# A later assumed landing for the gathers of softmax sums, in the scheduler of a fused attention and feed-forward kernel

## The chip, the cores and the metric

The kernel runs on one core of a Trainium2 chip. The metric is the device time of one execution in microseconds (us). The core's engines work side by side and meet through semaphores: PE (TensorE) multiplies matrices, with PEld its weight loads; DVE (VectorE), ACT (ScalarE) and POOL (GpSimd) do elementwise work; SP (SyncE) issues most DMAs. Each engine has one stream of instructions, with waits between them, so an instruction that waits holds up all that stands behind it in its stream.

## The reference, cut to what matters

```python
# q, k, v: (8, 12, 448, 64); w_in: (768, 2048); w_out: (2048, 768)
q_n = q / (norm(q) + 1e-6);  k_n = k / (norm(k) + 1e-6)
scores = q_n @ k_n.T / tau                    # 448 x 448 for each of 96 heads
attn = exp(scores - max) / sum(exp(scores - max))
x = (attn @ v) -> (3584, 768)                 # heads side by side
h = x @ w_in
out = (h * cos(h)) @ w_out
```

## The kernel before, in words

**The work.** The 96 heads are 48 pairs (called groups, g = 0 to 47); three groups make a unit (u = 0 to 15), two units a batch (b = 0 to 7). For a group, POOL squares q and k (L629), DVE sums the squares (L636, "red"), ACT makes the norms' reciprocals (Ln at L657, Exp at L660), POOL scales (L668, "scale"), and the result is transposed by a DMA on SP (L685, T9 to T47). PE computes the scores in four steps (L719 and L727, SCg.0 to SCg.3), ACT their exponentials (L734), and PE the product with v (L760, L767, L793) and, by columns of ones, the softmax sums (L775, L783). DVE (L850) or ACT (L847) copies both from PSUM to the buffer `xu`.

**The chain of a unit** (function `chain`, L884 to L911) then divides by the sums:

1. *gather* (L888, four DMAs on SP): the sums go from `xu` into a compact tile `sums`;
2. *sum* (L900) and *recip* (L903) on DVE, each a small instruction;
3. *spread* (L904, SP): the reciprocals go to DRAM;
4. *bcast* (L906, two DMAs on SP): they come back, repeated over partitions, as `RB`;
5. *x* (L910, POOL): one multiplication for each group gives `xT`, bf16.

Some groups ("direct": 9, 10, 11, 17, 23, 47 among the later ones) make their reciprocal on ACT (L873) and need no chain. Unit 2's sum and reciprocal run on POOL.

**The feed-forward part.** For a batch, M1 (L918) multiplies six tiles of `xT` with w_in, 16 steps of six matmuls; ACT takes the cosine (L947), DVE multiplies (L949, "g"). The first two pairs of steps run early over the first three tiles (the even unit's), then over the fourth, the fifth and the sixth (the odd unit's). M2 (L1016; in quarters of 64 by 64) multiplies with w_out and is cut into small pieces that fill PE's time between the attention steps; its PSUM bank, MP, is drained by two DVE copies ("osb", L983), and only then may the next tile of M2 begin. The outputs leave by DMAs on SP (L987).

**What sets the order.** The order on PE and of most ACT work follows a script written out by hand. For the other engines, a planner in the kernel (`Program.play`, L180 on) simulates all engines once with a cost for each operation, and each engine takes, among what is ready in this simulation, the operation that is due first. `Program.emit` writes the instructions in the simulated order of starts. A DMA's landing is modelled; `pad` is added to it for whoever waits for it (`latency`):

```python
    def latency(self, y, o):
        if y.dma is not None:
            return y.pad
```

The gather's pad comes from the plan:

```python
        dma("SP", [...], [("xs", i, p) for p in range(n)], [("sums", i)], "sums%d" % i, 0.7,
            "gather%d" % u, pad=0.0 if u in PLAN["power"] else PLAN["late"])
```

With `"late": 0.0` the planner lets a sum start as soon as the modelled gather has landed. `PLAN["rush"]` is a bias on the due time of one unit's sum and recip: unit 11 is given 3 us less. `PLAN["queue"]` fixes a few orders on SP beyond what the planner finds: T34 behind spread 9, T40 behind spread 11, T46 behind spread 13; out 11 behind bcast 9, out 15 behind bcast 11, out 18 behind bcast 13.

Of the kernel before, what the change touches and what calls it, by code (L numbers as in the profile page):

```python
# [14 lines left out]
    "apart": 1,  # L15
    "ahead": (1, 2),
    "hurry": {2: -8},
    "rush": {11: -3},
    "swapped": {},
    "script": {19: """  # L20
        s19.0 f5 s19.1 f4 s19.2 f6 s19.3 f6 a18 f4 b18 s20.0 c18 c19
# [27 lines left out]
    "v3": (7, ("xa", 2, 0)),  # L49
    "late4": {2: (7, "T9")},  # L50
    "power": (2,),
    "late": 0.0,
    "mixed": (3, (3, 0, 1, 2, 0, 1, 2, 0), (2, 3, 4, 0, 1, 5)),
    "turned": 9,
    "first": (3, 1, 2, 0, 3, 1, 2, 0),
# [359 lines left out]
def bass_cosine_attention__then__act_gcu_kernel(  # L415
# [13 lines left out]
    UP = 3  # L429
# [156 lines left out]
    def load(u, p0, p1, apart=False, eng="SP", behind=None, reads=()):  # L586
        i = u % 2
        h = slice(2 * p0, 2 * p1)
        f = [lambda e, x=x, t=t: e.dma_start(
            rawv[i][BP * x : BP * x + BP, h].rearrange("p h s d -> p h (s d)"), src(t, u, 2 * p0, 2 * (p1 - p0)))  # L590
            for x, t in enumerate((k, q))]
        for x in ((0,), (1,)) if apart else ((0, 1),):
            behind = P.ops[-1] if x == (1,) else behind
            dma(eng, [f[y] for y in x], list(reads), [("raw", i, p, y) for p in range(p0, p1) for y in x] + (["first"] if (u, p0) == (0, 0) and 1 in x else []),
                "raw%d_%d_%s" % (i, p0, x), 0.97 * (p1 - p0) * len(x), "load u%d p%d" % (u, p0), behind, 1.8,
                pad=LATE if u > 1 else 0.0)
# [328 lines left out]
    def m1(b, early=0, split=NKC, turn=TURN, order=tuple(range(NKC)), done=0, inner={}):  # L925
        table(SINSET)

        def names(gi):
            return BANKS.get(PHs[turn[gi]][0], [PHs[turn[gi]][0]])

        def step(gi, a, c0, c1):
            m1_step(b, turn[gi], 2 * gi + a, c0, c1, order)

        for gi in range(done):
            for a in range(2):
                step(gi, a, NKC - 2, NKC - 1)
        for c0, c1 in [(0, split)] + [(c, c + 1) for c in range(split, NKC - 1)]:
            for gi in range(done, early):
                for a in range(2):
                    step(gi, a, c0, c1)  # L940
        for gi in range(NF // 2):
            for g in inner.get(gi, ()):
                transposes(g)
            ph, cz = PHs[turn[gi]][1], gi % 2
            for a in range(2):
                step(gi, a, NKC - 1 if gi < early else 0, NKC)
            act(lambda e, ph=ph, cz=cz: e.activation(cosv[cz], ph[:, :, 0:S], ACT.Sin, bias=cst.ap()[:, 0:1], scale=1.0),  # L947
                names(gi) + ["cst0"], [("cos", cz)], 2 * S, "S", 1, label="sin%d.%d" % (b, gi))
            dve(lambda e, ph=ph, cz=cz, gi=gi: e.tensor_tensor(  # L949
                gTv[:, 2 * gi : 2 * gi + 2, S * (b % 2) : S * (b % 2) + S], ph[:, :, 0:S], cosv[cz], ALU.mult),  # L950
                names(gi) + [("cos", cz)], [("gT", b % 2, gi)], 2 * S, label="g%d.%d" % (b, gi))
        table(EXPSET)
# [13 lines left out]
    def m2_add(b):  # L966
        for t in range((b * S) // 128, ((b + 1) * S) // 128):
            w = [0, HW, DM]
            if t == B * S // 128 - 1 and PLAN["tail"]:
                w.insert(2, HW + PLAN["tail"])  # L970
            for hf, x in enumerate(zip(w, w[1:])):
                m2_queue.append([t, hf, 0, None, x])
# [57 lines left out]
    def m2_fill(n, quarters=False):  # L1030
        while n > 0 and (m2_queue or m2_tile):
            if m2_tile or quarters and m2_queue[0][1:3] == [0, 0]:
                n -= m2_quarters(n)
                continue
            t, hf, f, bank, w = item = m2_queue[0]
            if bank is None:
                bank = item[3] = banks[0][nhalf[0] % len(banks[0])]
                nhalf[0] += 1
            name, po = bank
            col = (128 * t) % RING  # L1040
            m = min(4, n, NF - f)

            def go(e, po=po, f=f, m=m, col=col, w=w):
                for y in range(f, f + m):
                    r = e.matmul(po[:, 0 : w[1] - w[0]], gTv[:, y, col : col + 128], W2v[:, y, w[0] : w[1]],  # L1045
                                 start=(y == 0), stop=(y == NF - 1))
                return r

            P.op("PE", go, gates(t, f, m), name, cost=m * ((w[1] - w[0]) / 2400.0 + 0.0025), mode="F", label="M2 %d" % t)
            item[2] = f + m  # L1050
            n -= m
            if f + m == NF:
                m2_queue.pop(0)
                m2_drain(t, hf, name, po, w)
            elif f + m == NF - PLAN["twin"] and t == (B - 1) * S // 128 and not hf:
                m2_queue[0:2] = m2_queue[1::-1]
            elif f + m == NF - PLAN["twin"] and t == (B - 1) * S // 128:
                m2_queue[0:2] = m2_queue[1::-1]
# [21 lines left out]
    def find(label):  # L1080
        return [o for o in P.ops if o.label == label][-1]
# [23 lines left out]
    def direct(g):  # L1105
        return g in PLAN["direct"]

    def loads(u, behind=None, reads=()):
        if u < NU:
            for p in range(UP):  # L1110
                load(u, p, p + 1, behind=behind, reads=reads)
# [14 lines left out]
    def ahead_norms(g):  # L1126
        u, p = g // UP, g % UP
        if 3 <= u < NU - 1:
            if p == 0:
                norms(u + 1, 0)  # L1130
            if p == u % 2:
                norms(u + 1, 1)

    def unit_done(g):
        u = g // UP
        if g > PB and not direct(g - 1) and (g % UP == 0 or direct(g)):
            chain((g - 1) // UP)
        if g % UP == 0:
            if g > PB and (u <= 3 or u % 2 == 0):
                for x in range(UP if u + 2 < NU else 0):  # L1140
                    load(u + 2, x, x + 1, behind=find("bcast%d" % (2 if u == 4 else u - 1)) if u > 3 else
                         find(PLAN["u5"][x]) if u == 3 else None)
            if g > PB:
                for x, y in PLAN["vloads"].get(u, [(u + 2, "x%d" % (g - 1 if u % 2 == 0 else g - 4))]):
                    load_v(x, find(y))

    def play(text):
        order, phase, last = [0, 2, 1], {}, 0

        def touch(x=None):  # L1150
            x = [y for y in order if y not in [held[z] for z in phase if len(phase[z]) < 3]][0] if x is None else x
            order.remove(x)
            order.append(x)
            return x

        for w in text.split():
            kind, rest_ = w[0], w[1:]
            if kind == "o":
                order[:] = [int(x) for x in rest_]
                continue  # L1160
            if kind == "f":
                m2_fill(int(rest_), True)
                continue
            if kind == "m":
                m1(int(rest_), 2, UP, tuple(touch() for x in range(NF // 2)))
                m2_add(int(rest_))
                continue
            if kind == "s":
                g, c = (int(x) for x in rest_.rstrip("=").split("."))
                if c == 0:  # L1170
                    ahead_norms(g)
                last = touch(last if rest_[-1] == "=" else None)
                scores(g, c, last)
                if c == 1 and max(TD, PB + 2) <= g + 2 < NG:
                    transposes(g + 2)
                if c == 3 and g % UP == UP - 1 and g // UP % 2 == 0:
                    loads(g // UP + 3, find("bcast%d" % (g // UP - 1)))
                continue
            g = int(rest_)
            held[g] = touch(held.get(g))  # L1180
            if kind == "c" and g not in phase:
                turned.add(g)
            attend(g, direct(g), ({"a": 0, "b": 1, "c": 2}[kind],))
            phase[g] = phase.get(g, "") + kind
            if len(phase[g]) == 3:
                unit_done(g + 1)
# [164 lines left out]
```

## Time and profile before

| what | value |
|---|---|
| median of 3 runs (lowest to highest) | 421.99 us (420.87 to 422.92) |
| the profiled execution | 421.52 us, of which the span of its instructions 419.8 us |
| PE busy | 411.3 us, 98% of the span |
| DVE, ACT, POOL busy | 188.8, 272.1, 242.8 us |
| granted TensorE clock | 1.0 in every slice |
| DMA | 152 GB/s in the mean |

"Busy" is the time in which an engine had an instruction in work; matmuls are pipelined, so PE's share is an upper bound of its use. A wait is shown as idle time of an engine with the instruction that ended it. The span has 40 slices, and PE's row shows 9 tenths or more in all but the first, the second and the last. The chain that ended last, followed back through the whole span, is 87% PE, 4% ACT, 3% DMA, 2% POOL and 1% DVE.

### The profile page before, as it was taken

The page shows a single profiled execution, that of the slowest core. Times are in us where ns is not written, and L with a number is a line of the kernel's source. Part 1 is how long each engine was busy: PE and PEld are TensorE (multiplying, and loading weights), DVE is VectorE, ACT ScalarE, POOL GpSimd, SP SyncE. Part 2 cuts the span into 40 slices and gives each one's busy share as a digit, 9 for nine tenths or more (in the row PEclk, how much of TensorE's full clock was granted, in tenths as well). Part 3 has the DMA queues.
Part 4 walks back from the last instruction along what each step waited for, and adds up shares of the span by engine and source line. Part 5 has one row for each costly group of instructions (what it writes and reads, how often), then busy time and mean ns, then how long its engine had stood idle before and what let it go on. Part 6 is the DMA issues. An engine that isn't in the chain of part 4 may idle for free.

```text
span 419.8 us, 13605 instructions
## 1 busy us (share of the span) xinstructions
PE 411.3 (98%) x6077; PEld 236.9 (56%) x6077; DVE 188.8 (45%) x250; ACT 272.1 (65%) x363; POOL 242.8 (58%) x193
## 2 busy tenths in 40 slices
PE   8899999999999999999999999999999999999996
PEld 3454556655566555665566555665566655555555
DVE  3564744356743277124752087213862244223421
ACT  4897578984987646876598556776498645703500
POOL 4999977998941866938864684808957302020000
PEclk9999999999999999999999999999999999999999
DMA  8999999999966998789665994759936920141023
GB/s 185 251 255 226 207 220 187 207 216 154 157 100 129 231 180 172 147 182 218 153 122 114 210 250 100 124 117 221 240 89 89 187 68 2 42 121 38 2 71 81
DMA packets 81034, 63.61 MB, mean 152 GB/s; under 512 B 45776, under 2 KB 75984, under 8 KB 80976
## 3 DMA queue, kind: packets, MB, share of 16 engines
q1 hardware_dynamic: 62768, 50.06, 57.3%
q0 software_dynamic: 18048, 12.59, 20.6%
q8 instruction: 48, 0.79, 0.8%
q10 hardware_dynamic: 160, 0.10, 0.1%
q14 instruction: 10, 0.08, 0.1%
HBM read 54.98 MB, written 11.13 MB: 157 GB/s over the span
## 4 chain that ended last, share of the span: by engine, by line
PE 87%; ACT 4%; DMA 3%; POOL 2%; SPq 2%; DVE 1%; issue 0%; ACTq 0%; POOLq 0%
PE MP L1016 25%; PE SC L918 21%; PE AV L918 11%; PE SC L719 6%; PE AV L767 4%; PE MP L1045 4%; PE SC L1045 3%; PE AV L793 2%; ACT PX L734 2%; PE SC L767 2%; PE AV L760 2%; PE MP L918 2%; DMA sums<-xu 1%; DMA raw<-in_q_dram 1%; POOL qks L668 1%; ACT cosb L947 1%
## 5 line engine op out<-in xcount | busy, mean ns | idle before, releaser
L734 ACT ACTIVATE PX<-SC 128x896 bf16<-128x896 f32 (+1 forms) x166 | 132.7, 828 | 25.2 <-PE SC L719 17.7
L1016 PE MATMUL MP<-W,gT 64*64 64x384 bf16 x2816 | 142.4, 324 | 1.3 <-DVE qkT L706 0.6
L1016 PEld LDWEIGHTS MP<-W,gT 64*64 64x64 bf16 x2816 | 78.8, 107 | 37.0 <-PE MP L1016 4.3
L918 PE MATMUL SC<-xT,W 128*128 128x448 bf16 x468 | 94.9, 353 | 0.0
L668 POOL TENSOR_TENSOR qks<-raw,rn 128x896 bf16<-128x896 f32 (+1 forms) x48 | 79.7, 1677 | 23.9 <-ACT rn L660 23.3
L629 POOL TENSOR_TENSOR sq<-raw 128x896 bf16<-128x896 f32 x44 | 73.4, 1688 | 9.7 <-DMA raw<-in_q_dram 7.6
L947 ACT ACTIVATE cosb<-SC,cst 128x896 f32<-128x896 f32 x39 | 39.1, 1006 | 57.0 <-PE SC L918 51.3
L910 POOL TENSOR_TENSOR xT<-xu,RB 128x448 bf16<-128x448 f32 x34 | 37.8, 1134 | 64.6 <-DMA RB<-scr 64.6
L918 PEld LDWEIGHTS SC<-xT,W 128*128 128x128 bf16 x468 | 45.5, 98 | 42.8 <-ACT xu L847 0.6
L949 DVE TENSOR_TENSOR gT<-SC,cosb 128x896 bf16<-128x896 f32 x39 | 42.4, 1089 | 39.7 <-ACT cosb L947 37.4
L918 PE MATMUL AV<-xT,W 128*128 128x448 bf16 x264 | 56.7, 353 | 0.0
L636 DVE TENSOR_REDUCE n<-sq 128x14 f32<-128x896 bf16 (+2 forms) x49 | 51.3, 1057 | 6.2 <-ACT sq L627 5.6
L983 DVE COPY osb<-MP 128x384 f32<-128x384 f32 x50 | 25.7, 548 | 57.4 <-PE MP L1016 46.8
L719 PE MATMUL SC<-qkT 64*64 64x448 bf16 x504 | 45.9, 356 | 0.6 <-ACT PX L734 0.4
L918 PEld LDWEIGHTS AV<-xT,W 128*128 128x128 bf16 x264 | 25.6, 98 | 24.2 <-ACT xu L847 0.3
L947 ACT ACTIVATE cosb<-AV,cst 128x896 f32<-128x896 f32 x22 | 22.1, 1006 | 23.6 <-PE AV L918 20.7
L949 DVE TENSOR_TENSOR gT<-AV,cosb 128x896 bf16<-128x896 f32 x22 | 23.9, 1085 | 13.0 <-ACT cosb L947 13.0
L603 POOL DMA_DIRECT2D va<-in_v_dram x32 | 21.9, 689 | 8.0 <-DMA raw<-in_q_dram 4.2
L877 POOL TENSOR_TENSOR xT<-xu,RB 128x448 bf16<-128x448 f32 x8 | 9.1, 1134 | 26.1 <-ACT RB L873 26.1
L850 DVE COPY xu<-AV 128x896 f32<-128x896 f32 x13 | 14.1, 1086 | 20.3 <-PE AV L783 14.4
L719 PEld LDWEIGHTS SC<-qkT 64*64 64x64 bf16 x504 | 14.6, 105 | 14.4 <-ACT PX L734 6.4
L734 ACT ACTIVATE PX<-AV 128x896 bf16<-128x896 f32 (+1 forms) x26 | 21.1, 811 | 2.3 <-PE AV L719 1.4
(95 smaller groups left out, 430.3 us busy)
## 6 DMA issues: line engine op xcount, KB each, us to landing
raw<-in_k_dram SPq DMA_DIRECT2D x48, 224.0 KB, 6.6
raw<-in_q_dram SPq DMA_DIRECT2D x48, 224.0 KB, 7.2
out_dram<-osb SPq DMA_DIRECT2D x54, 192.0 KB, 3.8
va<-in_v_dram POOLq DMA_DIRECT2D x32, 192.0 KB, 8.7
RB<-scr SPq DMA_DIRECT2D x18, 336.0 KB, 4.8
W<-in_moe_w_in_dram POOLq DMA_DIRECT2D x4, 768.0 KB, 14.9
W<-in_moe_w_out_dram POOLq DMA_DIRECT2D x4, 768.0 KB, 19.8
RB<-scr SPq DMA_DIRECT2D x6, 224.0 KB, 4.4
```

Source lines behind the costliest of these rows:

```text
L629: pool(lambda e, x=x, y=y: e.tensor_tensor(y, x, x, ALU.mult), src_, dst, 0.1 + n * 1.78e-3, label="sq%d.%d" % (u, p)).pad = LATE if u > 1 ...
L636: dve(lambda e, w=w: e.tensor_reduce(out=n2v[i][:, 2 * p : 2 * p + 2, w], in_=sqv[p][:, :, w, :], axis=mybir.AxisListType.X, op=ALU.add), ...
L668: f = lambda e, s0=s0, s1=s1: e.tensor_tensor(qksv[i][:, p, s0:s1].rearrange("p s h d -> p h s d"), rawv[i][:, h, s0:s1, :], bass.AP(rn[i] ...
L719: m = e.matmul(ph[BP * o : BP * o + BP, a, 0:S], t[r, c - 1 + (NT3 + 1) * o, 0:BP], t[r, :, BP : 2 * BP], start=True, stop=True)
L734: act(lambda e: e.activation(PHv[j] if c == 0 else PXv[j][:, c - 1], ph[:, :, 0:n], ACT.Exp, scale=1.0 / TAU), keys, [("PX", j, c)], 2 * n ...
L910: pool(lambda e, p=p: e.tensor_tensor(xTv[b % 2][:, UP * i + p, :], xuv[:, u % 3, p, :], RBv[i][:, p, :], ALU.mult), [("RB", i, p), ("xa", ...
L918: t = e.matmul(ph[:, a, 0:S], W1v[:, order[c], 128 * n : 128 * n + 128], xTv[b % 2][:, order[c], :], start=(c == 0), stop=(c == NKC - 1))
L947: act(lambda e, ph=ph, cz=cz: e.activation(cosv[cz], ph[:, :, 0:S], ACT.Sin, bias=cst.ap()[:, 0:1], scale=1.0), names(gi) + ["cst0"], [("c ...
L949: dve(lambda e, ph=ph, cz=cz, gi=gi: e.tensor_tensor(gTv[:, 2 * gi : 2 * gi + 2, S * (b % 2) : S * (b % 2) + S], ph[:, :, 0:S], cosv[cz], ...
L983: dve(lambda e: e.tensor_copy(dst, po[:, 0:n]), name, [("osb", o, hf)], n, label="osb%d" % t)
L1016: r = e.matmul(POH[b][x : x + 64, 0:HW], gTv[k, y, col + x : col + x + 64], W2v[k, y, HW * b : HW * b + HW], start=(y == 0 and h == 0), st ...
L1045: r = e.matmul(po[:, 0 : w[1] - w[0]], gTv[:, y, col : col + 128], W2v[:, y, w[0] : w[1]], start=(y == 0), stop=(y == NF - 1))
```

## The change

Two entries of the plan and one line of the script's reader:

```diff
-    "rush": {11: -3},
+    "rush": {},
...
-    "late": 0.0,
+    "late": 1.0,
...
                 if c == 3 and g % UP == UP - 1 and g // UP % 2 == 0:
-                    loads(g // UP + 3, find("bcast%d" % (g // UP - 1)))
+                    loads(g // UP + 3, find("bcast%d" % (g // UP - 1)) if g // UP > 4 else None)
```

The planner now counts each gather (units 4 to 15; unit 2 has its own rule) as landed 1.0 us later than before, and unit 11's sum has no bias. The third edit stands in the reader of the script, which starts at group 19 (unit 6), so its condition holds there always.

No operation is added, removed or altered in size. PE's and ACT's instructions stand in the same order in both programs; those of DVE, POOL and SP do not. Of the order on DVE, this differs:

| chain | before | after |
|---|---|---|
| 4 | sum, recip, xu 16, osb 4 | xu 16, sum, recip, osb 4 |
| 6 | red 9.0, g 2.6, sum, recip, g 2.7, xu 21, red 9.1, red 9.2 | g 2.6, red 9.0, sum, g 2.7, xu 21, red 9.1, red 9.2, recip |
| 7 | sum, recip, osb 8 twice | osb 8 twice, sum, recip |
| 8 | red 10.0, g 3.2, red 10.1, g 3.3, red 10.2, g 3.4, g 3.5, sum, recip, g 3.6, red 11.0, g 3.7, xu 27 | g 3.2, red 10.0, g 3.3, red 10.1, g 3.4, g 3.5, sum, g 3.6, red 10.2, recip, g 3.7, xu 27, red 11.0 |
| 9 | sum, recip, osb 11 twice | osb 11 twice, sum, recip |
| 10 | red 12.0, g 4.2, red 12.1, ... g 4.5, sum, recip, red 13.1, g 4.6, g 4.7, red 13.2 | g 4.2, red 12.0, g 4.3, ... g 4.6, red 13.1, sum, g 4.7, red 13.2, recip |
| 11 | sum, recip, osb 15 twice | osb 15 twice, sum, recip |
| 13 | sum, recip, osb 18 twice | osb 18 twice, sum, recip |
| 15 | sum, osb 21, recip, osb 21 | osb 21 twice, sum, recip |

Chains 5, 12 and 14 keep their places. On SP the order follows: gather 5 stands before spread 4; T24 before spread 6 and T25 before bcast 6; out 8 before spread 7 and T28 between spread 7 and bcast 7; out 7 behind gather 7; T36 before bcast 10 and T37 behind it; T47 before out 18; out 21 before spread 15. On POOL: scale 9.1 and 9.2 before x 18, the load of v for unit 11 before x 21, the power of unit 10 (L653, L654) before the third square, scale 11.0 before x 25, scale 13.1 and 13.2 before x 30, the load of v for unit 15 behind the squares of unit 15.

## The prediction

> **What bounds the kernel now.** I read the busy shares first, then the list of waits, then the idle time of PE alone, then the chain of work that ended last around it, and last the SP and POOL streams ahead of each M1.
>
> ```profile
> PE 411.3 (98%) x6077; PEld 236.9 (56%) x6077; DVE 188.8 (45%) x250; ACT 272.1 (65%) x363; POOL 242.8 (58%) x193
> ```
>
> PE is the bound: 411.3 of 419.8 us. PE's order is unchanged, so the change can only take away PE's waits or add some. The list of waits (us in total, times, longest) has what the edit aims at, and what it may touch:
>
> ```profile
> POOL xT L910 <- DMA RB<-scr: 64.6, 9, 13.7
> ...
> DVE rcp L900 <- DMA sums<-xu: 32.0, 9, 5.8
> ```
>
> DVE stands idle for 32.0 us in nine sums. But DVE is 45% busy, so this counts only where PE waits for something queued behind a sum. The timeline of PE shows three idle times in all of 112 to 376 us (in brackets: idle before, releaser):
>
> ```profile
> 277.43 0.84 PE L1016 MATMUL MP<-W,gT 64*64 64x384 bf16 x16 [0.33 <-DVE osb L983]
> 309.65 0.38 PE L719 MATMUL SC<-qkT 64*64 64x448 bf16 x4 [0.19 <-ACT PX L734]
> 324.53 0.52 PE L1016 MATMUL MP<-W,gT 64*64 64x384 bf16 x8 [0.17 <-DVE osb L983]
> ```
>
> Two are PE waiting for a drain of M2's bank, and the chain of work shows why the drain was late (start, length):
>
> ```profile
> 273.04 2.92 DMA sums<-xu
> 275.96 0.02 issue
> 275.98 0.21 DVE rcp L900
> 276.19 0.02 issue
> 276.21 0.04 DVE rcp L903
> 276.25 0.17 issue
> 276.42 0.96 DVE osb L983 x2
> 277.38 0.04 issue
> 277.43 0.84 PE MP L1016 x16
> ```
>
> The gather of unit 11 lands at 275.96, and two drains that need nothing from it stand behind its sum. At 320.00 to 324.53 the same rows stand for unit 13.
>
> **What it removes.** No instruction is added or removed, and no duration changes. At chains 7, 9, 11, 13 and 15 both drains now stand ahead of the sum. Unit 11: the tile's last matmuls start at 274.58 and take 1.15, to 275.73; the drain at 267.10 began 0.12 after such an end (266.32 + 0.66). So the drains run from 275.85 to 276.85, and PE, which asks at 277.43 - 0.33 = 277.10, waits no more: -0.33. Unit 13: last matmuls 321.55 + 0.49 = 322.04, drains done by 323.2, PE asks at 324.36: -0.17. What is late next there is nothing that the trace shows: PE's next idle time, the 0.19 at 309.65, is ACT's and stays. Elsewhere the waits end with PE busy. Sum: **-0.50**.
>
> The matmul rows may hide some loss, since their ends are modelled. The weight loads sat idle for 0.60 and 0.44 at the two places, so -1.04 is the far end; I take -0.50, what PE itself shows. The Trainium skill (Perfetto Trace Analysis, Identifying the Most-Contended Engine) says that matmul busy time is a poor measure of headroom on TensorE and that the weight loads are a better one. By that rule the sum would be the far end.
>
> **What it adds.** A sum behind two drains comes later, and so do its spread and bcast on SP, and the multiplications that PE's next M1 needs. I went through all nine moved chains.
>
> Odd units, wanted soon. Block b's M1 takes 12 steps of 0.189 (2.27 for 12 in the chain of work) before it wants the first odd tile, then 0.75 for each further one.
> - Unit 9: drains free at 224.76, done about 225.85, sum 225.59 to 225.85: +0.3. x is done at 237.7 and first wanted at 239.2 (M1 from 236.9): hidden.
> - Unit 11: +0.8; tiles done at 286.6, 287.7, 288.8, wanted at 288.8, 289.6, 290.3 (M1 from 286.56): 1.5 spare, hidden.
> - Unit 13: drains done when the gather lands (323.06): 0.
> - Unit 15: spread now behind both drains and out 21, 368.00 to about 369.6, +1.6; tiles done at 376.6 and 377.7, wanted at 379.9 and 380.7: 3.0 spare, hidden.
> - Unit 7 is the narrow one. On SP:
>
> ```profile
> 179.55 0.34 SPq L904 DMA_DIRECT2D scr<-rcp  x1
> 180.62 1.14 SPq L987 DMA_DIRECT2D out_dram<-osb  x2
> 181.81 1.25 SPq L906 DMA_DIRECT2D RB<-scr  x2
> ```
> and on POOL, the two tiles of unit 7:
> ```profile
> 189.62 2.23 POOL L910 TENSOR_TENSOR xT<-xu,RB 128x448 bf16<-128x448 f32 x2 [7.94 <-DMA RB<-scr]
> ```
>
> M1 starts at 189.93 and wants them at 192.21 and 192.96; they are done at 190.75 and 191.85, 1.1 to spare. In the new order: drains 179.57 to 180.6, sum and recip to 181.1, out 8 180.62 to 181.76, spread 7 181.8, T28 (free when SC25.3 ends, 181.85) 182.2 to 183.45, bcast 7 at 183.45 instead of 181.81: **+1.64**. Its second half is issued 0.6 later, at 184.05. Second halves ahead of other M1s landed 4.7 (unit 5), 5.8 (unit 9), 6.3 (unit 11), 5.7 (unit 13) and, here, 7.1 after their issue:
>
> ```profile
> DMA to landing us min/median/max: 6.1/6.6/7.1
> ```
>
> So RB lands between 188.75 and 191.15. The multiplications end 0.12 + 2.23 = 2.35 later, and PE stalls by (landing - 190.61) if that is above 0: 0 to 0.54. The load of v for unit 11, now ahead on POOL, is free when group 26's first products end (188.8) and takes 1.34: x can't start before 190.2, which still costs nothing. T28 ahead in SP's stream is a cost that the trace of before does not show: nothing at best, at worst all of the shortest transpose (2.6 from issue to landing; landing 193.75, a stall of 3.1). Its 0.23 MB (128 x 896 in bf16) at the 255 GB/s that moved from 187 to 189 is 0.9, landing up to 192.1, a stall of 1.5. I take 6.3, the second longest row, because bcast 7 no longer starts together with the load of v issued at 180.34: landing 190.4, **stall 0**, and keep 0 to 3.1.
>
> Even units, wanted a block later: spread 4 now stands behind gather 5, at about 129.1 instead of 123.33, but bcast 4 only moves from 131.14 to 132.6, x 12 from 136.98 to 138.5, wanted at 143.49. Unit 6's bcast moves by some 4.5, unit 8's by 2, unit 10's by 6; their tiles end by 180, 223 and 272, wanted at 189.9, 236.9 and 286.6. Transposes moved later (T27 by 0.7, T30 by 3.4 behind POOL's power, T34 and T40 by under 1) are wanted 7 us or more after their issue.
>
> ACT's stream takes Ln rows that wait for DVE's reductions, ahead of exponentials that PE needs. Red 10.2 ends near 209.2 for the Ln at 211.12, red 11.2 near 214.5 for 217.07, red 13.2 near 258.5 for 259.21: 0.7 at the narrowest, covered; without cover one reduction, 1.08, at most. The g rows of M1 come earlier or stay.
>
> **Sum.** 421.52 - 0.50 + 0 = 421.0 in the profiled execution's own time. That run is 0.47 below the median of the three shown; on the median's scale **421.5**.
>
> **Rivals.**
> - *PE waits for unit 7's tiles by 0.5 to 1.6* (landing 191.1 to 192.2): net 0 to +1.1, 422.0 to 423.1. For it: bcast 7 has the longest landing of all already, and T28 now goes first. Against: the load of v has a head start of 1.6.
> - *Slower: the whole of T28 is paid ahead of bcast 7.* Landing 193.75, net -0.50 + 3.1 = +2.6: **424.6**. It decides from a landing at 190.6 on and outweighs the gain from 191.1 on. The Trainium skill (DMA: Bandwidth & Descriptors, Queues, rings and completion order) says that each DMA engine consumes a ring's descriptors in order, and that a completion is written only after all earlier writes of that engine. By that rule T28 would delay bcast 7; the trace of before has no transpose just ahead of it and does not show how much.
> - *The change doesn't do what it says:* a drain ahead of the sum meets the same wait elsewhere, or PE's 0.5 returns at the next bank. Then 422.0, within 0.2.
> - *Faster by over 2.1:* only if matmul rows hide waits that no idle time shows; three idle times sum to 0.69.
>
> **How the numbers follow.** A measurement of this kernel can tell about 0.5%, 2.1 us, from no change (the three runs differ by 2.05). Forecast 0.57, tiles late by up to 1.6 0.25, T28 paid in full 0.08, nothing moves 0.06, faster 0.04. Slower by over 0.5% (above 424.1) takes the T28 case and a little of the one before: 0.10. Faster (below 419.9): 0.05. Within: 0.85. The forecast's own range is 421.0 (the far end of the gain) to 422.0. The range goes to 423.1 for the late tiles, and by 0.4 beyond both ends for the medians' scatter: 420.6 to 423.5.
>
> **What would show it.** PE's idle times at 277 and 324 gone, the sums of units 7, 9, 11 behind their drains, DVE's wait for gathers well under 32.0; bcast 7 issued near 183.4, and no idle time of PE from 192 to 193.5. Wrong would be an idle PE there with x of unit 7 as releaser, or a stall in front of the exponentials near 259.

## The result, and the profile after

The changed kernel takes **424.56 us** in the median of 11 runs (422.37 to 424.84), the kernel before 421.99 us beside it: a ratio of **1.0051 [1.0036, 1.0065]**. A second time, on another chip, the ratio was 1.0031 [1.0005, 1.0058]. The forecast was 421.5, no change, with a range that ended at 423.5. Executions at a granted clock of 0.992 to 0.996 last up to 431 us: e1, e2 and e3 below have four, five and four of them among ten runs, which draws their ratios up (the medians of their other runs are 422.8, 422.4 and 422.8 us, beside 422.4 for the kernel before), and the profiled execution of e1 is one of them, so its losses stand in brackets.

The profiled execution took 424.56 us, its span is 422.8 us. First the busy shares on its page, then the two rows of the list of waits (us in total, times, longest) that answer to those of before.

```profile
PE 410.8 (97%) x6077; PEld 236.4 (56%) x6077; DVE 189.2 (45%) x250; ACT 272.2 (64%) x363; POOL 242.8 (57%) x193
```
```profile
POOL xT L910 <- DMA RB<-scr: 63.0, 10, 13.7
DVE rcp L900 <- DMA sums<-xu: 12.4, 4, 5.4
```

No engine has more work to speak of: PE's 410.8 is 0.5 less than before and DVE's 189.2 is 0.4 more, while the span is 3.0 longer. DVE's wait for gathers fell from 32.0 to 12.4 us, which is what the edit does. So the loss is idle time of PE. These are PE's idle times in the timeline from 65 us on (in brackets: idle before, releaser):

```profile
167.12 0.38 PE L719 MATMUL AV<-qkT 64*64 64x448 bf16 x4 [2.12 <-DVE gT L949]
195.21 0.55 PE L918 MATMUL AV<-xT,W 128*128 128x448 bf16 x2 [0.81 <-POOL xT L910]
196.29 0.55 PE L918 MATMUL AV<-xT,W 128*128 128x448 bf16 x2 [0.16 <-POOL xT L910]
214.66 0.38 PE L719 MATMUL SC<-qkT 64*64 64x448 bf16 x4 [0.38 <-ACT PX L734]
313.12 0.38 PE L719 MATMUL SC<-qkT 64*64 64x448 bf16 x4 [0.19 <-ACT PX L734]
```

The two waits for drains at 277 and 324 are gone, as forecast. Four others have come, all of them before 215 us (the one at 313 is that of 309.65 before). PE's order is the same in both programs, so each place can be weighed by the start of the same matmuls (the first scores of each group, line 727), after less before:

| from group to group | after less before | what lies there |
|---|---|---|
| up to 22 | 0.0 | |
| 22 to 23 | +2.02 | unit 6: PE waits for g 2.7 |
| 27 to 28 | +1.33 | unit 7: M1 waits for x 21 and x 22 |
| 28 to 29 | +0.63 | unit 8: scores that wait for ACT's exponential (ends at 214.57) and for the bank of g 3.7 (ends at 214.52) |
| 37 to 38 | -0.51 | unit 11: the drain no longer waits |
| 44 to 45 | -0.36 | unit 13: the same |
| sum | +3.11 | the times differ by 424.56 - 421.52 = 3.04 |

**Unit 6** in the chain of work that ended last (start, length):

```profile
153.09 12.66 DMA sums<-xu
...
165.77 0.04 DVE rcp L900
...
165.89 1.09 DVE gT L949
...
167.12 0.38 PE AV L719 x4
```

The row is the last of the gather's four parts, 5.2 KB each, and it takes 12.66 us: on SP they were issued behind the twelve loads of raw q and k for units 8 and 9. Its sum stands in front of g 2.7 on DVE, and PE's scores of group 22 need the bank that g 2.7 empties. Before the change the same gather took as long. These are the times from issue to landing of its four parts, before and after (lowest, median, highest):

```profile
DMA to landing us min/median/max: 11.9/12.3/12.9
```
```profile
DMA to landing us min/median/max: 12.1/12.5/12.7
```

But SP issued it 2.26 us later. These are SP's rows before the change, from bcast 4 to spread 5 and out 4, and the gather:

```profile
131.14 1.23 SPq L906 DMA_DIRECT2D RB<-scr  x2
132.41 0.59 SPq L904 DMA_DIRECT2D scr<-rcp  x1
133.05 1.15 SPq L987 DMA_DIRECT2D out_dram<-osb  x2
...
148.96 2.46 SPq L888 DMA_DIRECT2D sums<-xu  x4
```

After it out 4 comes first:

```profile
130.42 2.33 SPq L987 DMA_DIRECT2D out_dram<-osb  x2
132.80 1.24 SPq L906 DMA_DIRECT2D RB<-scr  x2
134.08 0.59 SPq L904 DMA_DIRECT2D scr<-rcp  x1
...
151.22 2.46 SPq L888 DMA_DIRECT2D sums<-xu  x4
```

Before, g 2.7 began at 163.20 and no row of PE shows a wait for it:

```profile
163.20 1.03 DVE L949 TENSOR_TENSOR gT<-AV,cosb 128x896 bf16<-128x896 f32 x1
```

**Unit 7**, on SP after the change (start, length of the issue), then in the chain:

```profile
182.65 1.10 SPq L987 DMA_DIRECT2D out_dram<-osb  x2
183.80 1.63 SPq L904 DMA_DIRECT2D scr<-rcp  x1
185.52 1.25 SPq L685 DMA_TRANSPOSE qkT<-qks  x1
189.30 1.52 SPq L906 DMA_DIRECT2D RB<-scr  x2
```
```profile
183.80 5.49 DMA scr<-rcp
...
189.82 4.13 DMA RB<-scr
...
194.03 2.22 POOL xT L910 x2
```

Spread 7 (L904) is a few KB. It was issued at 179.55 before and landed 1.5 us later; now it stands behind out 8 (L987) and takes 5.49. Bcast 7 (L906) waits for that landing and is issued at 189.30 instead of 181.81. T28 (L685) goes out while SP would wait anyway: bcast 7 follows within 0.02 us of the landing.

### The profile page after: what moved, and what is told of

It reads as the page before. It is cut to its first block, busy times and chain, and to the rows that moved or that the text cites. A ratio compares the mean times of both kernels' runs of the same rounds, so it can differ in the third digit from the quotient of the medians.

```text
span 422.8 us, 13603 instructions
## 1 busy us (share of the span) xinstructions
PE 410.8 (97%) x6077; PEld 236.4 (56%) x6077; DVE 189.2 (45%) x250; ACT 272.2 (64%) x363; POOL 242.8 (57%) x193
## 4 chain that ended last, share of the span: by engine, by line
PE 83%; DMA 6%; ACT 4%; POOL 3%; DVE 2%; SPq 1%; issue 1%; ACTq 0%; DVEq 0%; POOLq 0%
PE MP L1016 24%; PE SC L918 19%; PE AV L918 10%; PE SC L719 6%; PE AV L767 4%; PE MP L1045 4%; DMA sums<-xu 3%; PE SC L1045 3%; PE AV L793 2%; PE AV L760 2%; PE MP L918 2%; PE SC L767 2%; POOL qks L668 1%; ACT cosb L947 1%; ACT PX L734 1%; DMA scr<-rcp 1%
```

## The experiments

The theory drawn from these two traces, the **slip**: spread 4 behind gather 5 makes SP's stream late, the small transfers then queue behind bulk ones, and PE pays at units 6 and 7. Rivals: DVE's order at unit 6; at unit 7 the price of T28, or of DVE's order.

Two numbers from each profile decide. "Loss" is the growth of the offset of the groups' starts against the kernel before, from group 21 to 23 (unit 6) and 27 to 28 (unit 7). T23 is the transposition that stands between the loads of unit 8 and unit 9 on SP, with its time from issue to landing.

| kernel | ratio [interval] | T23 lands after | loss unit 6 | loss unit 7 |
|---|---|---|---|---|
| before | 1 | 11.2 | 0 | 0 |
| changed | 1.0051 [1.0036, 1.0065] | 11.2 | 2.02 | 1.33 |
| e1, late at unit 4 only | 1.0034 [1.0001, 1.0067] | 11.3 | (4.69) | (0.37) |
| e2, spread 4 first | 1.0053 [1.0017, 1.0089] | 8.0 | 0.0 | 1.68 |
| e3, sum 6 behind g 2.7 | 1.0044 [1.0013, 1.0076] | 10.0 | 0.5 | 2.01 |
| e4, late at 11 and 13 only | 0.9981 [0.9960, 1.0002] | 11.1 | 0.23 | 0.0 |
| e5, changed, again | 1.0031 [1.0005, 1.0058] | 9.2 | 1.05 | 1.29 |
| e6, late from unit 5 on | 1.0002 [0.9980, 1.0025] | 7.7 | -0.3 | 1.13 |
| e7, spread 7 first | 1.0046 [1.0024, 1.0067] | 6.6 | 0.4 | 2.06 |
| e8, bcast 7 before T28 | 1.0026 [1.0005, 1.0047] | 11.5 | 2.10 | 1.62 (0.94 of it unit 7) |
| e9, e7 and e8 together | 1.0009 [0.9978, 1.0039] | 8.4 | -0.3 | 0.0 |
| e10, late at unit 7 only | 1.0019 [0.9995, 1.0044] | 11.4 | -0.3 | 1.33 |
| e11, recip 7 first | 0.9996 [0.9978, 1.0013] | 12.1 | 3.06 | 0.0 |
| e12, e4 again | 0.9970 [0.9951, 0.9989] | 7.6 | -0.3 | 0.0 |
| e13, out 4 and spread 4 back | 1.0050 [1.0031, 1.0068] | 7.6 | 0.0 | 3.10 |
| e14, out 4 early only | 1.0034 [1.0012, 1.0056] | 9.4 | 0.65 | 0.0 |
| e15, e13 and e9 together | 0.9995 [0.9980, 1.0011] | 8.1 | 0.5 | 0.0 |

Each loss is that of one execution. Losses of unit 6 up to 0.65 are small waits beside it (x 16; a load of v, 0.41 in e14), and not PE waiting for g 2.7, but for the 0.23 of e4. The -0.3 that many rows have is 0.29 by which the kernel before is late from group 22 to 23; no idle row shows why. In e8 only 0.94 of the 1.62 is PE waiting for x 21 and x 22. The rest lies ahead of the first scores of group 28, which wait for g 3.6, and that stands behind unit 8's sum and its gather.

### e1: the later landing for unit 4 alone

```diff
 # the kernel before
-    "late": 0.0,
+    "late": {4: 1.0},
```

Where `late` is a table, here and below, a unit that it doesn't name gets 0.0, as before the change.

> The kernel before, with unit 4's gather alone counted 1.0 us later. On DVE this moves chain 4 behind xu 16 and, as its consequence, chain 6; on SP spread 4 goes behind gather 5. Theory (slip): spread 4 moves bcast 5, the loads of units 8 and 9 and gather 6 behind them; gather 6 lands about 3 us later than before, DVE's sum of unit 6 holds g 2.7 behind it, and PE stalls by 2.0 to 2.2 near 167 us. So most of the loss comes from this one entry: +1.8 to +2.3 against before, with the 0.33 and 0.17 at 277 and 324 still there. Rival (late tiles): the loss comes from T28 ahead of bcast 7 and the chains behind it; then this kernel is within 0.5 of before.

Measured: 1.0034 [1.0001, 1.0067]. In the profiled execution PE waits 2.34 us for g 2.7 at 168.60, as in the changed kernel, though nothing at units 5 to 15 was asked to be later. For the reason given with the result, this makes it likely that unit 4 alone brings the wait of unit 6, and doesn't show it. Unit 7 can't be read from it.

### e2: spread 4 ahead of gather 5

```diff
 # the changed kernel
     ("spread4", "gather5")   # added to PLAN["queue"]
```


> The changed kernel, with spread 4 put back ahead of gather 5 on SP (bcast 4 then stands ahead of out 4); DVE, POOL, PE and ACT keep the changed order. Theory (slip): bcast 5 is issued near 137.6 instead of 139.2, gather 6 near 149 instead of 151.2, its sum starts by 163 and PE's 2.12 at 167 is gone; the stalls for unit 7's tiles and behind the third M1 may stay. -1.7 to -2.2 against the changed kernel. Rival (DVE's own order around g 2.6, red 9.0 and the sum makes the wait): it stays at +2 to +3 over before.

Measured: no wait at 167, and unit 7 lost 1.68. That looked like a proof and wasn't one: gather 6 was still issued at 151.62, as late as in the changed kernel. It landed early, as T23 did (8.0 us). Spread 4's place is not what makes SP late.

### e3: sum 6 behind g 2.7 on DVE

```diff
 # the changed kernel
     ("g2.7", "sum6")   # added to PLAN["queue"]
```


> The changed kernel, with unit 6's sum put behind g 2.7, xu 21 and red 9.1 on DVE; all other streams keep the changed order, so gather 6 is as late as in the changed kernel (lands near 165.8). Theory (slip, paid through DVE's stream): g 2.7 starts near 163, PE's 2.12 at 167 is gone though the gather is as late; -1.7 to -2.1 against the changed kernel. Rival (the late gather is paid through the tiles of unit 6, not through DVE's stream): the wait moves and the time stays within 0.5 of the changed kernel.

Measured: no wait for g 2.7, with T23 slow (10.0) and gather 6 issued at 151.82. g 2.7 began at 163.85, as soon as ACT had its cos. So it is the sum ahead of it on DVE that hands the gather's lateness to PE (the sum stands ahead of g 2.7 in the kernel before, too). Unit 7 lost 2.01.

### e4 and e12: the later landing for units 11 and 13 alone

```diff
 # the kernel before
-    "rush": {11: -3},
+    "rush": {},
-    "late": 0.0,
+    "late": {11: 1.0, 13: 1.0},
```


> The kernel before, with only the gathers of units 11 and 13 counted 1.0 us later (and unit 11's bias taken away): both drains stand ahead of the sums of units 11 and 13, nothing moves before 270 us. Theory: PE's 0.33 at 277 and 0.17 at 324 are gone and nothing is added: -0.5, 0.1% (between -0.2 and -0.9). Rival (the waits return at the next bank): within 0.1 of before, with new idle times of PE behind 277.

> The kernel with the later landing for units 11 and 13 alone once more, on another chip, since its interval reached 1.0 by a hair: the two waits at 277 and 324 are gone (0.5 and 0.36 us by the groups' starts), nothing is lost at units 6 and 7 beyond 0 to 0.4 us. Ratio 0.997 to 0.999; if it is 1.000 or more, the gain of the two waits is not seen in the time.

Measured: 0.9981 [0.9960, 1.0002] and, on another chip, 0.9970 [0.9951, 0.9989]. The two waits for drains go and the groups' starts gain 0.51 and 0.36. This is the part of the change that does what it is for, and e12's is the only interval here that lies below 1. Nothing ahead of 270 us is ordered otherwise than in the kernel before, and yet gather 6 is issued at 150.61 and 150.51 here on that kernel's scale (each start less the run's offset at group 21), and not at 148.96: an order that stays the same scatters by 1.65 us at this place, and the 0.23 that e4 loses at unit 6 comes from no edit.

### e5: the changed kernel again

> The changed kernel once more, beside the kernel before on one chip, as an anchor for the edits made to it. All theories: about 1.004 to 1.006 of the kernel before, with TensorE waits of about 2 us between 162 and 168 us (gather 6) and of about 1.3 us in the x21/x22 groups of unit 7 (194 to 197 us). If these waits come and go from run to run, the theory that they are the whole of the loss is weaker.

Measured: 1.0031 [1.0005, 1.0058]; 1.05 lost at unit 6, 1.29 at unit 7, nothing at unit 8. So unit 6's loss differs from execution to execution, and the 0.63 of unit 8 comes and goes. Unit 7's is alike in these two, but e2, e3 and e13, which keep the changed orders of unit 7 on SP, lose 1.68, 2.01 and 3.10 there, with spread 7 landing 4.1, 4.0 and 7.5 us after its issue.

### e6: the later landing from unit 5 on

```diff
 # the changed kernel
-    "late": 1.0,
+    "late": {5: 1.0, 6: 1.0, ... 15: 1.0},
```


> The later landing is counted from unit 5 on only, so gather 4, spread 4 and with them spread 6 stand on SP as before the change; the moves of units 9, 11, 13 and 15 stay, and T28 still stands ahead of bcast 7. Slip theory (SP's stream slips behind gather 5, gather 6 and spread 7 then land late): the 2.0 us at 167 and the 1.3 us at 195 both go, the gains of 0.5 and 0.4 at 277 and 324 stay, so 0.997 to 1.000 of before (420.8 to 422). Rival (T28 ahead of bcast 7, or recip 7 behind osb 8, is what costs 1.3 us): about 1.001 to 1.002, with 1.0 to 1.5 us idle at x21. Rival (the orders of units 9 and later cost it): 1.004 to 1.005 as the changed kernel.

Measured: 1.0002 [0.9980, 1.0025]. Unit 6 lost nothing (with a fast T23), the gains of 0.5 and 0.36 stayed, unit 7 lost 1.13. The slip theory said that unit 7's loss would go too. That part of it fell: spread 7 stands ahead of out 8 here and is issued at 180.79, 1.2 later than before, it lands 4.2 us after that, and bcast 7 still goes only at 185.49, behind T28. (Out 4 stands ahead of spread 5 in e6, as in the changed kernel.)

### e7, e8, e9: spread 7 and bcast 7, one at a time and both

```diff
 # the changed kernel, added to PLAN["queue"]
     ("spread7", "out8")                        # e7
     ("bcast7", "T28")                          # e8
     ("spread7", "out8"), ("bcast7", "T28")     # e9
```


> The changed kernel with one order more: spread 7 ahead of output transfer out 8 on SP, as before the change (a few orders of unit 8 move with it). Slip theory with out 8 as the bulk ahead of spread 7: spread 7 lands 1.5 to 2.5 us after its issue in place of 5.5, the 1.3 us idle at x21 and x22 go, the 2.0 us at 167 stay: about 1.002 to 1.004 of before. Rival (out 7, load v or the slip itself hold spread 7): idle at x21 stays 0.8 to 1.4 us, ratio 1.004 to 1.006.

> The changed kernel with T28 behind bcast 7 on SP. Slip theory: T28 is issued while SP waits for spread 7 to land, so nothing moves: bcast 7 is issued within 0.3 us of spread 7's landing as in the changed kernel and 1.0 to 1.4 us stay idle at x21 and x22; ratio 1.004 to 1.006. Rival of the prediction (T28's transfer is paid in full ahead of bcast 7's): the idle time at x21 falls below 0.3 us and the time falls by about 1.3 us, to 1.001 to 1.003.

> The changed kernel with both SP orders of unit 7 as before the change: spread 7 ahead of out 8, bcast 7 ahead of T28. Sum 7 and recip 7 stay behind osb 8 on DVE. Each of the two alone left 1.1 to 2.0 us lost between the groups 27 and 28. If SP's two orders together make the loss (each alone is made good by the other), the loss at group 28 is below 0.4 us, the tile RB of unit 7 lands within 7 us of bcast 7's issue, and the ratio is 0.999 to 1.003, according to what unit 6 costs (0 to 2 us). Rival (DVE's order, sum 7 and recip 7 behind osb 8, is enough by itself): 0.5 to 1.3 us at group 28, ratio 1.001 to 1.005.

Measured: e7 2.06 (0.34 of it an idle time of PE that nothing ends, "issue"), e8 1.62, e9 0.0. Either order alone leaves a loss, both together take it, in e9 and once more in e15. SP of e9 (in this kernel line numbers are one higher):

```profile
181.35 0.34 SPq L905 DMA_DIRECT2D scr<-rcp  x1
181.74 1.72 SPq L988 DMA_DIRECT2D out_dram<-osb  x2
184.27 1.11 SPq L907 DMA_DIRECT2D RB<-scr  x2
```
and POOL's unit 7:
```profile
190.70 2.22 POOL L911 TENSOR_TENSOR xT<-xu,RB 128x448 bf16<-128x448 f32 x2 [7.14 <-DMA RB<-scr]
```

Bcast 7 goes at 184.27, x 21 starts at 190.70, and PE waits for nothing. DVE's order at unit 7 is still the changed one here, so that rival fell. In e7 spread 7 lands after 1.7 us, but T28's issue at 182.82 takes 2.18 and bcast 7 only goes at 185.05. In e8 T28 is out of the way, but spread 7 behind out 8 lands after 5.4. In each of the two, one holds what the other would have held.

### e10 and e11: unit 7 alone, and all but unit 7

```diff
 # e10, the kernel before
-    "late": 0.0,
+    "late": {7: 1.0},
 # e11, the changed kernel, added to PLAN["queue"]
     ("recip7", "osb8")
```


> The kernel before with the later landing counted for unit 7 alone: sum 7 ahead of osb 8 and recip 7 behind it, T28 ahead of bcast 7, spread 7 ahead of out 8 as before; unit 6 and SP ahead of it unchanged. If unit 7 costs by itself: 1.0 to 2.0 us lost between the groups 27 and 28, 0 to 0.4 at group 23, the waits of 0.3 and 0.2 at 278 and 325 still there: ratio 1.002 to 1.004. Slip theory in its first form (unit 7 is late only because SP's stream is late since unit 4): below 0.3 us at group 28, ratio 0.999 to 1.001.

> The changed kernel with recip 7 ahead of osb 8 on DVE; the planner then also puts sum 7, spread 7 and bcast 7 back where they were before the change (ahead of osb 8, out 8 and T28), and red10 of unit 8 too. Unit 6 stays as changed. Both theories of unit 7: nothing lost at group 28 (below 0.3 us). What is left is unit 6: 0 to 2.1 us at group 23, less 0.9 us for the two waits that go at 277 and 324: ratio 0.998 to 1.002. If 1 us or more is lost at group 28 all the same, the slip since unit 4 is what makes unit 7 late.

Measured: e10 loses 1.33 at unit 7 and nothing at unit 6, without a slip at unit 4; with recip 7 ahead of osb 8 the planner puts spread 7 and bcast 7 back, and e11 loses nothing there, with the largest loss at unit 6 outside the brackets (3.06). So neither loss needs the other. SP and PE of e10:

```profile
180.44 0.34 SPq L904 DMA_DIRECT2D scr<-rcp  x1
180.83 3.30 SPq L987 DMA_DIRECT2D out_dram<-osb  x2
184.23 1.29 SPq L685 DMA_TRANSPOSE qkT<-qks  x1
185.57 1.23 SPq L906 DMA_DIRECT2D RB<-scr  x2
```
```profile
192.85 0.55 PE L918 MATMUL AV<-xT,W 128*128 128x448 bf16 x2 [0.82 <-POOL xT L910]
```

### e13, e14, e15: SP ahead of unit 6

```diff
 # added to PLAN["queue"]
     ("spread4", "gather5"), ("spread5", "out4")   # e13, the changed kernel
     ("out4", "spread5")                           # e14, the kernel before
     ("spread4", "gather5"), ("spread5", "out4"),
     ("spread7", "out8"), ("bcast7", "T28")        # e15, the changed kernel
```


> The changed kernel with nothing moved but SP's order ahead of unit 6: spread 4 ahead of gather 5 again, and out 4 behind bcast 4 and spread 5 and T22's place again, as before the change. If the output transfer out 4 ahead of spread 5 is what makes SP's stream slip: bcast 5 is issued near 138 in place of 139.2 to 140, gather 6 near 149 to 150 in place of 151 to 152.7, and at group 23 no more than 0.4 us is lost even where T23 lands over 9 us after its issue; unit 7's 1.1 to 2.0 us and the gains of 0.9 us stay: ratio 1.000 to 1.003. Rival (sum 6 and its neighbours in DVE's order, or chance, cost it at unit 6): gather 6 stays at 151 or 1 to 2 us are lost at group 23 with a slow T23: ratio 1.003 to 1.005.

> The kernel before with output transfer out 4 ahead of bcast 4 and spread 5 on SP (the planner then moves sum 6, red9.0, spread 6 and gather 7 as in the changed kernel; spread 4 stays ahead of gather 5, and unit 7 stays as before). If out 4 ahead of spread 5 makes the slip: spread 5 lands 4 us or more after its issue, bcast 5 is issued 1.2 us or more later than 137.6, gather 6 at 150.5 or later, and where T23 lands slowly 1 to 2.3 us are lost at group 23: on the average 0.5 to 1.3 us, ratio 1.001 to 1.003. If spread 4's place is what it takes: nothing at group 23, ratio 0.999 to 1.001.

> The changed kernel with five places of SP's order as before: spread 4, out 4, spread 7, bcast 7 and T28. Everything else that the change moved stays moved (orders of DVE at units 4 to 15 but for small moves in unit 8, SP's at units 6 and 8 to 15). If these places hold the whole loss: no more than 0.4 us lost at groups 23 and 28, 0.9 us gained at 277 and 324, ratio 0.997 to 0.999, as with the later landing for units 11 and 13 alone. Rival (other moved orders cost too, unit 8 above all): 1.000 to 1.002.

Measured: in e14 out 4 (issue: 2.32 us) stands ahead of bcast 4, spread 5 is issued at 134.75 instead of 132.41, bcast 5 at 139.82 instead of 137.64, gather 6 at 151.42 instead of 148.96, with spread 4 in its old place. That one output transfer makes the slip is borne out by all profiles but e1's together. With out 4 ahead of spread 5 (ten executions) gather 6 is issued at 150.67 to 152.70 on the scale of the kernel before, 151.5 in the mean; with out 4 behind it (before, e4, e10, e12, e13, e15) at 148.96 to 150.61, 149.9 in the mean. So the slip is about 1.6 us, and the 2.26 of the first pair holds scatter.

The profile of e14 doesn't price it: T23 was near the fast side (9.4), g 2.7 began at 164.51, just when PE, late by x 16 and a load of v, asked for it. The time says 1.0034 [1.0012, 1.0056], with unit 7 as before the change (sum 6, red 9.0, spread 6 and gather 7 moved, too). In e13 the slip is gone (gather 6 at 150.29, within the six above); T23 was fast, so e13 says nothing on what that saves. Its large loss at unit 7 has 1.19 of "issue" in it. e15 has no wait at 167, 195, 277 or 324. Its ratio, 0.9995 [0.9980, 1.0011], is no longer that of the changed kernel. Whether it reaches e12's 0.9970 can't be told: the intervals overlap.

The other times don't show a price of the slip: with unit 7 put right, e15 without it has 0.9995, e9 and e11 with it 1.0009 and 0.9996; with unit 7 as changed, e13 without it has 1.0050, the changed kernel 1.0051 and 1.0031. What putting unit 7 right saves is seen in the times, some 0.4% between these two groups.

**Unit 6 in one number.** On the scale of the kernel before (each start less that run's offset at group 21), the start of g 2.7 gives the loss in the executions in which T23 was slow and g 2.7 was what PE waited for, with two that had no such wait beside them:

| | before | e10 | e4 | e5 | changed | e8 | e11 |
|---|---|---|---|---|---|---|---|
| gather 6 issued | 148.96 | 149.17 | 150.61 | 151.67 | 151.21 | 152.08 | 152.70 |
| g 2.7 starts | 163.20 | 163.44 | 164.14 | 164.92 | 165.88 | 165.96 | 166.92 |
| loss | 0 | -0.3 | 0.23 | 1.05 | 2.02 | 2.10 | 3.06 |

From 163.86 on, loss = start - 163.86, to 0.05. So the kernel before had 0.66 us to spare at this place. With out 4 ahead of spread 5 and a slow T23 the loss is 1.05 to 3.06 (0.65 in e14, at 164.51; e3 has its sum elsewhere); with one of the two alone PE waits 0.23 at most for g 2.7. So the slip of SP goes with one part of the lateness and T23 with the other. What makes T23 land after 6.6 to 8.4 us in seven executions and after 9.2 to 12.1 in the rest stays open.

## Why the prediction was wrong, point by point

The sum put -0.50 for what goes and 0 for what comes. In the profiled executions -0.87 goes, and 2.02 (unit 6), 1.33 (unit 7) and 0.63 (unit 8) come: +3.11.

**The gain** had the right places and the wrong size: -0.50 in the sum, -0.51 - 0.36 = -0.87 measured. The idle rows of PE (0.33 and 0.17) show only a part of such a wait. The Trainium skill (Perfetto Trace Analysis, Identifying the Most-Contended Engine) holds the weight loads for a better measure than matmul busy time. The weight loads' idle times (0.60 and 0.44, the far end of -1.04) are nearer to what was measured than the rows that I took. The gain is also that of one execution of the kernel before: e10 and e14 keep its orders at units 11 and 13, and against them the same two places gain 0.42 and 0.08, or 0.44 and 0.55.

**Unit 4 is the step with the largest loss in the profile.** "Bcast 4 only moves from 131.14 to 132.6" was right (132.80), and I stopped there. Out 4 had moved ahead of bcast 4 in the same order, and I didn't follow it: spread 5 and bcast 5 come behind, the twelve loads behind bcast 5, and gather 6 behind the loads, 2.26 us later at the end (some 1.6 of it by the order, as the other profiles have it). **"The g rows of M1 come earlier or stay"** failed with it. That holds for DVE's order. It does not hold once the sum in front of them waits 2.99 us for a gather. Nowhere did I ask when gather 6 lands, and how much it had to spare.

**Unit 7** was named as the narrow one, its sign of being wrong (an idle PE with x of unit 7 as releaser) is what came, and its formula held. Stall = landing - 190.61, less the offset that PE already has, gives 1.32 for the changed kernel (193.95 - 190.61 - 2.02), 1.32 for e10, 2.06 for e7, 1.11 for e6, 3.08 for e13, 0.94 for e8 and nothing for e9, each within 0.03 of what PE loses there. The term that was wrong is bcast 7's issue, "183.45", measured as 189.30. The sum sends bcast 7 right behind T28, which leaves spread 7 1.65 us from issue to landing, as in the row of before (1.52), though in the new order out 8 stands right ahead of it. It took 5.49. The drains, too, came at 181.60 and not 179.57, since PE was 2.03 late.

**The rival "PE waits for unit 7's tiles by 0.5 to 1.6"** has the size of unit 7's stall, 1.33, and its releaser. Its way there was a landing of bcast 7 more than 7 us after an issue at 184.05; in the trace the issue is late (189.82) and the landing takes 4.13.

**The rival "the whole of T28 is paid"** gave 424.6, and the time is 424.56. That is chance: of 3.0 us only 1.33 lies at unit 7, and there T28 doesn't hold bcast 7 as long as spread 7 is late (with T28 ahead or, in e8, behind, bcast 7 goes within 0.02 us of that landing). Its mechanism shows where spread 7 is early: e7 and e9 differ by T28's place and a few moves of unit 8, and by 2.06 us, one execution of each. In e7 bcast 7's second half is issued 1.0 us later than in e9, on PE's scale, and lands after 7.2 instead of 5.9 us. That is less than the 3.1 set for it. The Trainium skill (DMA: Bandwidth & Descriptors, Queues, rings and completion order) says that each DMA engine consumes the descriptors of a ring in order. The traces fit this: the 5.2 KB parts of gather 6 land some 12.5 us after their issue behind bulk loads, and spread 7 lands after 4.0 to 7.5 us in the six executions in which it stands behind out 8 (e1 left out), and after 1.5 to 4.5 in the ten in which it stands ahead. I cited the rule for T28 and didn't apply it to the small transfers, which are the ones that the chain waits for.

**What held:** units 9, 11, 13 and 15 cost nothing, the Ln rows of ACT neither, and DVE's wait for gathers went well under 32.0. The 0.63 at unit 8 is not explained by a run of its own. In the trace gather 8 is issued at 201.73, before at 197.66; 3.35 of these 4.07 us is PE's own lateness by then, 0.72 is SP's. Its sum now waits 1.90 us for it on DVE, where it didn't wait before, and holds g 3.6 and with it g 3.7. That this is the cause is likely and not shown.

## What to carry to other kernels

When an order changes around small transfers, follow the queue that they are issued on to the next thing that an engine waits for, not to the next block: a gather of 5 KB costs what lies ahead of it. Put small transfers that a chain waits for ahead of bulk outputs and transposes that nobody waits for yet, and test such orders together, since undoing one of two may show nothing (e7, e8, e9). Take the scatter of a landing or of an issue from executions with the same order (before, e4, e10, e12) before a difference is put down to an edit. A planner's number that is raised everywhere to mend two places is better raised at these two (e12).

## What the runs showed of the hardware

T23 lands after 6.6 to 8.4 us or after 9.2 to 12.1, also with the same orders all around it (e4 11.1, e12 7.6). In all ten executions with a late T23 there are 2 to 4 us between 150 and 156 in which the DMA moves 47 to 120 GB/s; in the seven with an early one no 2 us there have less than 141. Here are the changed kernel, then e7 with a fast T23 (busy time of PE, PEld, DVE, ACT and POOL with the number of instructions, granted clock, DMA share, GB/s; the share adds up the packets' times and can pass 1):

```profile
152.00:154.00 2.00, 2.00 (x12) 1.06 (x11) 1.10 (x2) 1.01 (x1) 1.28 (x2) 1.00 1.75 89
```
```profile
152.00:154.00 2.00, 2.00 (x12) 1.06 (x11) 1.52 (x2) 0.74 (x2) 2.00 (x2) 1.00 1.29 235
```

89 GB/s at a share of 1.75 against 235 at 1.29. No run here tells what slows the packets. With gather 6 issued late and 0.66 us to spare, PE loses 1 to 3 us or nothing according to it. How much of the spread of the changed kernel's times it makes isn't shown: the kernel before spreads from 420.56 to 424.32 us beside e5.

A spread that stood ahead of out 8 landed after 1.5 (before), 1.7 (e7), 2.9 (e9), 4.2 (e6) and 4.5 us (e10): being first on SP does not fix the landing alone.

A wait of PE for a drain was longer than PE's idle row, and shorter than the idle row of the weight loads. Against the kernels in which the two waits for drains are gone, the waits cost 0.51 and 0.36 (before), 0.42 (e10) and 0.44 and 0.55 (e14) by the groups' starts. PE's idle rows are 0.33, 0.17, 0.24, 0.27 and 0.36, short by 0.17 to 0.19; the weight loads' are 0.60, 0.44, 0.51, 0.54 and 0.63, long by 0.08 to 0.10.
